# Queries loaded and cast by GpSimd's DMAs, two batches of queries turned by DMAs, and a new order of all events in an attention kernel fused with an ELU network

## The chip, the cores and the metric

The kernel runs on one core of one Trainium2 chip. A core has TensorE (PE in the profile), VectorE (DVE), ScalarE (ACT), GpSimd (POOL) and SyncE (SP), each with its own in-order queue, and 16 DMA engines that all queues share. The metric is the time of one execution on the device, in microseconds; lower is better. It is a median of three runs.

## The reference

Eight batches of eight heads, 576 positions, head size 64. Each batch and head has two attentions that are added, and the sum goes through a two-layer network with ELU.

```
q_d, k_d, v_d = mean over groups of 4 positions of q, k, v      # 144 positions
out_d    = softmax(q_d k_d^T / 8) v_d, each row repeated 4 times
out_local = softmax(q k^T / 8 where |i - j| < 4, else -1e9) v
x = (out_d + out_local) as 4608 tokens x 512
h = x @ w_in                                                    # 512 -> 2048
g = h if h > 0 else exp(h) - 1
y = g @ w_out                                                   # 2048 -> 512
```

## The kernel before

**Tiling.** Heads are taken in pairs, so there are 8 batches b of 4 pairs j. The tokens of the network are cut into 9 blocks t of 512; a batch has 576 tokens, so block t needs batch t and, from block 1 on, the end of batch t - 1.

**Attention of one (b, j).** `lq` loads q and k, `lv` loads v (four DMAs). The data must be 16-bit and have the head size on the partitions. There are three ways for this in the kernel before:

- Batches 0 and 1 (all but the first pair): `load_cast` (line 304). GpSimd issues DMAs that cast on the way, so a 16-bit tile `q16` or `k16` arrives (4 buffers each).
- All others: `load_qk` (line 313). SP issues DMAs of the 32-bit data to `q32` and `k32` (3 buffers each), and `cq` = `cast_qk` (line 335) casts them on GpSimd (line 344), each cast followed by a one-element copy `apart` (line 333).
- From 16 bits on: `tr` = `transposes` (line 399) turns tiles on TensorE into PSUM, and `eq`, `ek` = `evict` (line 422) copy them to `QT`, `KT`. A tile from a casting DMA takes 12 transposes of 64 columns (line 409), a cast tile takes 6 of 128 columns (line 414). From batch `FLIP` = 3 on k is turned by a DMA transpose instead: `fl` = `flip` (line 426), issued by SP. The same for q (`fq`) is written in the code from batch `FLIPQ` on, and `FLIPQ` is 8, so it does not occur.

A load for TensorE's transposes reads runs of 1536 bytes; a load for a DMA transpose reads runs of 256 bytes (`runs_` in `load_qk`).

Then `sq`, `sk` sum groups of four (on DVE, line 443, or in two steps on POOL, lines 447 and 452), `sc` makes the scores, `xl`, `xf` the exponentials (ACT, line 483), `mk` the mask (DVE), `dn` the denominators of a batch (TensorE, line 508), `rc` their reciprocals (DVE, line 518). These are spread over partitions by TensorE in batches 0 to 2 (`sp`, `sx`) and through DRAM in batches 3 to 7 (`so` writes, `si` reads back; both issued by SP). `cv` casts v (POOL), `vs`, `vd` sum it, `out` and `far` multiply with v, `nm` normalises (DVE), and `ad` adds both attentions into the block's input `xt` (line 650, on DVE for the triples in `CFG["adv"]`, else on POOL).

**Network of block t.** `m1.t.i` is one tile of 128 hidden units (4 matmuls of 512 columns, line 663); `ex` and `el` are the ELU, on ACT and DVE: for pairs (t, i) in `CFG["rl"]` two ACT steps and one DVE step (lines 680, 681, 690), else one ACT step and two DVE steps (683, 694, 695). `m2.t.i` is 4 matmuls of the second layer (line 708), `cp` copies and stores. The weights are cast by GpSimd's DMAs as well (`wi`, `wo`, four each of 512 KB).

**What sets the order.** All engines are in order, and the order of their instructions is one written list of events, `ORDER`; each event puts its instructions at the end of its engines' queues. An event written too late in the list comes earlier if something needs it, which is rare here (3 of 1281 events). PSUM tiles of the kind `two` have 3 buffers, and 2 after `cf`. `CFG` says which engine takes which copy, and `fill` how many matmuls on zeros TensorE runs ahead of some events (`keep`, line 394); 13 more stand at the start.

Of the kernel before, what the change touches and what calls it, by code (L numbers as in the profile page):

```python
# [127 lines left out]
lv.1.1 vd.0.0 sp.0.2 sx.0.2 lq.2.0 out.0.0 far.0.0 nm.0.0 ek.1.0 ad.0.0.1 out.0.2 lq.2.3 vs.0.1 vd.0.1
vs.0.3 far.0.2 ad.0.0.0 vd.0.3 sp.0.3 sx.0.3 cf out.0.1 nm.0.2 far.0.1 out.0.3 far.0.3 ad.0.2.0 mp.0.0
mp.1.0 nm.0.1 nm.0.3 ad.0.3.1 ad.0.1.0 mp.0.1 mp.1.1 ad.0.3.0 mp.0.2 mp.0.3 mp.1.2 sk.1.0 m1.0.0 ex.0.0  # L130
mp.1.3 m1.0.1 el.0.0 ex.0.1 el.0.1 tr.1.1 tr.1.3 m1.0.2 eq.1.1 ek.1.3 sq.1.1 ex.0.2 eq.1.3 m1.0.3 ek.1.1
sc.1.0 el.0.2 sq.1.3 m1.0.4 ex.0.3 el.0.3 m1.0.5 cq.2.1 xl.1.0 xf.1.0 cv.1.0 wi.3 ex.0.4 ex.0.5 tr.1.2
# [797 lines left out]
```

## Time and profile before

| what | value |
|---|---|
| median of 3 runs (lowest to highest) | 342.64 us (340.46 to 343.32) |
| the profiled execution's own time | 342.38 us |
| its span, first to last instruction | 340.6 us |
| mean granted TensorE clock | 0.99 |

The page is one profiled execution. Its first part gives each engine's busy time; its second cuts the span in 40 slices of 8.5 us and shows the busy share of each in tenths. Matmuls overlap, so TensorE's busy time is not all work at full rate. The groups by line give the mean duration of one instruction, and the idle time of the engine just before it. The chain of waits follows the work that ended last back from the end.

### The profile page before, as it was taken

Reading aid. Unit: us, or ns where it says so; the run is one execution under the profiler, and the core shown is the slowest. Engines: PE = TensorE matmul, PEld = TensorE weight load, DVE = VectorE, ACT = ScalarE, POOL = GpSimd, SP = SyncE. Lnnn points to the kernel's source line nnn. Section 1 sums busy time; section 2 is a strip of 40 time slices with the busy share of each in tenths; the row PEclk is TensorE's granted clock in tenths of the full one; section 3 lists DMA queues with packets and bytes.
Section 4 is the critical chain, followed back from the end, with each engine's and each line's share of the span. In section 5 each row is a group of like instructions: output and inputs, shape, how many; then the busy total and the mean of one; then the engine's idle time right before and its main releaser. Section 6 shows DMA issues by size and latency. Waiting matters only on the chain.

```text
span 340.6 us, 9762 instructions
## 1 busy us (share of the span) xinstructions
PE 325.0 (95%) x3976; PEld 169.8 (50%) x3976; DVE 230.7 (68%) x429; ACT 209.4 (61%) x365; POOL 156.5 (46%) x299
## 2 busy tenths in 40 slices
PE   6799979999999997999999999999999999999996
PEld 3355445555545553555555555555444444444443
DVE  2668998768778957788997966699775455443400
ACT  3544888888457862555676767765446646657621
POOL 6694765876795674857684347632011000000000
PEclk9879999999999999999999999999999999999999
DMA  8999999989887949999996996331310100000112
GB/s 168 195 180 227 168 248 224 196 196 155 214 149 165 232 114 179 249 199 224 166 251 152 162 239 169 115 88 69 89 64 31 63 34 31 31 33 31 56 70 92
DMA packets 99735, 48.66 MB, mean 143 GB/s; under 512 B 81130, under 2 KB 94698, under 8 KB 99690
## 3 DMA queue, kind: packets, MB, share of 16 engines
q1 hardware_dynamic: 93530, 41.57, 55.1%
q0 software_dynamic: 5600, 6.26, 11.4%
q8 instruction: 31, 0.51, 0.7%
q10 hardware_dynamic: 560, 0.21, 0.3%
q14 instruction: 14, 0.11, 0.1%
HBM read 41.66 MB, written 9.67 MB: 151 GB/s over the span
## 4 chain that ended last, share of the span: by engine, by line
PE 66%; DMA 15%; DVE 8%; ACT 3%; SPq 3%; issue 2%; POOL 1%; ACTq 0%; POOLq 0%; DVEq 0%
PE op L708 28%; PE hp L663 28%; DMA v<-in_v_dram 4%; DMA rcb<-rd 3%; DMA k<-in_k_dram 3%; DMA kt<-k 3%; DVE gt L695 2%; PE lg L592 2%; DVE rc L518 1%; SPq L427 1%; PE sc L463 1%; DVE e L694 1%; DVE ln L643 1%; DMA MASK<-MASKc 1%; PE den L508 1%
## 5 line engine op out<-in xcount | busy, mean ns | idle before, releaser
L663 PE MATMUL hp<-xt,WI 128*128 128x512 f16 x576 | 148.0, 380 | 2.5 <-DVE gt L695 2.2
L708 PE MATMUL op<-WO,gt 128*128 128x512 f16 (+2 forms) x592 | 145.3, 374 | 0.0
L663 PEld LDWEIGHTS <-WI 128*128 128x128 f16 x576 | 62.6, 114 | 57.3 <-issue 3.6
L708 PEld LDWEIGHTS <-gt 128*128 128x128 f16 x592 | 55.1, 98 | 60.2
L690 DVE SCALAR_TENSOR_TENSOR gt<-e,hp 128x512 f16<-128x512 f16 x71 | 48.4, 683 | 43.0 <-ACT e L681 42.6
L683 ACT ACTIVATE e<-hp 128x512 f16<-128x512 f32 x73 | 43.6, 599 | 41.5 <-PE hp L663 40.0
L680 ACT ACTIVATE r<-hp 128x512 f32<-128x512 f32 x71 | 42.6, 600 | 40.9 <-PE hp L663 40.5
L695 DVE SCALAR_TENSOR_TENSOR gt<-hp,e 128x512 f16<-128x512 f32 x73 | 50.5, 692 | 2.8
L650 POOL TENSOR_TENSOR xt<-ln 128x320 f16<-128x320 f16 (+7 forms) x35 | 25.8, 750 | 44.9 <-DVE ln L643 44.8
L681 ACT ACTIVATE e<-r 128x512 f16<-128x512 f32 x71 | 44.7, 630 | 2.2
L483 ACT ACTIVATE pex<-sc 128x580 f16<-128x580 f32 (+1 forms) x64 | 35.2, 591 | 11.3 <-PE sc L473 11.2
L694 DVE TENSOR_SCALAR e<-e 128x512 f16<-128x512 f16 x73 | 27.3, 374 | 20.3 <-ACT e L683 20.2
L386 POOL CAST v<-v 128x640 f16<-128x640 f32 x32 | 23.6, 738 | 13.4 <-DMA v<-in_v_dram 7.2
L716 ACT COPY os<-op 128x512 f32<-128x512 f32 (+2 forms) x37 | 21.1, 573 | 12.6 <-PE op L708 12.3
L643 DVE TENSOR_TENSOR ln<-lg,rcb 128x580 f16<-128x580 f32 x32 | 24.1, 752 | 0.0
L344 POOL CAST k<-k 96x768 f16<-96x768 f32 x24 | 19.6, 818 | 9.1 <-DMA k<-in_k_dram 9.1
L447 POOL TENSOR_TENSOR t<-qt 128x288 f32<-128x288 f16 x19 | 12.8, 672 | 23.6 <-ACT qt L424 13.1
L492 DVE TENSOR_TENSOR pex<-pex,MASK 128x580 f16<-128x580 f16 x32 | 19.6, 626 | 2.4 <-ACT pex L483 2.2
L344 POOL CAST q<-q 96x768 f16<-96x768 f32 x24 | 19.6, 817 | 0.0
L424 ACT COPY qt<-tqk 128x576 f16<-128x576 f16 x18 | 11.5, 637 | 5.9 <-PE tqk L414 5.0
L447 POOL TENSOR_TENSOR t<-kt 128x290 f32<-128x290 f16 x17 | 11.9, 703 | 6.8 <-DMA kt<-k 5.4
L638 DVE TENSOR_TENSOR ln<-lg,rcb 128x144 f16<-128x144 f32 x32 | 9.6, 300 | 7.7 <-PE lg L611 3.7
(71 smaller groups left out, 292.6 us busy)
## 6 DMA issues: line engine op xcount, KB each, us to landing
v<-in_v_dram SPq DMA_DIRECT2D x126, 80.0 KB, 4.2
out_dram<-os SPq DMA_DIRECT2D x35, 256.0 KB, 2.7
q<-in_q_dram SPq DMA_DIRECT2D x25, 288.0 KB, 4.9
k<-in_k_dram SPq DMA_DIRECT2D x25, 288.0 KB, 5.0
rcb<-rd SPq DMA_DIRECT2D x10, 362.0 KB, 5.4
WI<-in_moe_w_in_dram POOLq DMA_DIRECT2D x4, 512.0 KB, 10.7
WO<-in_moe_w_out_dram POOLq DMA_DIRECT2D x4, 512.0 KB, 7.5
q<-in_q_dram POOLq DMA_DIRECT2D x7, 144.0 KB, 6.8
```

The source lines that it names most:

```text
L344: nc.gpsimd.tensor_copy(out=x[:], in_=src)
L483: nc.scalar.activation(out=s["p"][:, :, a : a + n], in_=g2(s["sc"], a, n), func=AF.Exp, scale=SCALE / 16 if far else SCALE,)
L643: nc.vector.tensor_tensor(**near)
L650: eng.tensor_tensor(out=xt(t)[:, j, t0 - TBLK * t : t1 - TBLK * t], in0=ln[:, a:z], in1=_rep4(ln[:, ga : ga + (z - a) // 4]), op=AB.add,)
L663: nc.tensor.matmul(hps[(t, fc)][:], w_in(dc, fc), xts[t][:, dc, :], start=(dc == 0), stop=(dc == DMC - 1),)
L680: nc.scalar.activation(out=r[:], in_=hp[:], func=AF.Relu, scale=-1.0)
L681: nc.scalar.activation(out=e[:], in_=r[:], func=AF.Exp, scale=-1.0)
L683: nc.scalar.activation(out=e[:], in_=hp[:], func=AF.Exp)
L690: nc.vector.scalar_tensor_tensor(out=gts[t][:, fc, :], in0=e[:], scalar=-1.0, op0=AB.add, in1=hp[:], op1=AB.max)
L694: nc.vector.tensor_scalar(out=e[:], in0=e[:], scalar1=1.0, scalar2=-1.0, op0=AB.min, op1=AB.add)
L695: nc.vector.scalar_tensor_tensor(out=gts[t][:, fc, :], in0=hp[:], scalar=0.0, op0=AB.max, in1=e[:], op1=AB.add)
L708: nc.tensor.matmul(op_[:, a:z], gts[t][:, fc, 128 * tt : 128 * tt + 128], WO[fc // 4][:, fc % 4, a:z], start=(fc == 0), stop=(fc == FCN - 1),)
```

## The change

- `is_cast` now holds for batch 2 as well: q and k of batch 2 come by casting DMAs of GpSimd.
- `is_cast_q` holds for batches 3 to 5: q comes by a casting DMA of its own event `lc`, while `lq` loads k alone on SP, and `cq` casts k alone.
- `FLIPQ` is 6: q of batches 6 and 7 is loaded in runs of 256 bytes and turned by DMA transposes (`fq`, SP); it has no `tr` and no `eq`.
- The tables of engines, `adv` (29 entries to 20), `rl` (71 to 55), `fill` (31 matmuls to 30) and the whole list `ORDER` are other ones.

```diff
-FLIPQ = 8
+CASTQ = 6
+FLIPQ = 6
...
- 'eq': {0: 'DDAD', 2: 'DAAD', 4: 'AADD', 5: 'DDDA', 6: 'ADAA', 7: 'AADA', -1: 'DAAA'},
- 'ek': {1: 'ADAA', -1: 'AAAA'},
- 'sq': {1: 'DPDP', 2: 'DPPP', 3: 'PDDD', 4: 'PPPP', 5: 'PPDP', 6: 'DPDP', -1: 'DPPD'},
- 'sk': {0: 'PDDD', 1: 'DDPD', 2: 'PDPP', 4: 'DDDP', 6: 'DPDP', 7: 'DPPP', -1: 'PPDP'},
- 'vd': {0: 'AADA', 3: 'D', 5: 'D', 6: 'D', -1: 'A'},
- 'sx': {2: 'DAAD', -1: 'AAAA'},
+ 'eq': {1: 'AADA', 2: 'AAAD', 3: 'DAAD', 4: 'ADAA', 5: 'DADA', -1: 'AAAA'},
+ 'ek': {1: 'ADAA', -1: 'DAAA'},
+ 'sq': {1: 'DPDP', 2: 'PPPD', 5: 'PPPD', 6: 'DPPP', 7: 'DDPP', -1: 'PPDD'},
+ 'sk': {0: 'DDDD', 3: 'DDPD', 4: 'PPPD', 5: 'PDDP', 6: 'PDPD', -1: 'DPPP'},
+ 'vd': {0: 'AADA', 4: 'D', 5: 'D', -1: 'A'},
+ 'sx': {1: 'DAAA', 2: 'DDAD', -1: 'DADA'},
...
- 'fill': {('sc', 0, 0): 5,
-          ('sc', 0, 1): 3,
-          ('dn', 0, 0): 5,
-          ('sc', 0, 3): 2,
-          ('dn', 0, 1): 4,
-          ('sp', 0, 2): 2,
-          ('out', 0, 0): 3,
+ 'fill': {('sc', 0, 0): 4,
+          ('dn', 0, 0): 7,
+          ('sp', 0, 0): 2,
+          ('out', 0, 0): 5,
+          ('sp', 0, 1): 4,
           ('mp', 0, 0): 3,
-          ('mp', 1, 0): 2,
-          ('sc', 1, 0): 1,
-          ('sp', 1, 2): 1},
+          ('mp', 1, 0): 1,
+          ('dn', 1, 0): 2,
+          ('sp', 1, 2): 2},
...
     def is_cast(b, j):
-        return b < 2 and (b, j) != (0, 0)
+        return b < 3 and (b, j) != (0, 0)
+
+    def is_cast_q(b):
+        return 3 <= b < CASTQ
...
         for src, name in ((q, "q"), (k, "k")):
+            if name == "q" and is_cast_q(b):
+                got.append(None)
+                continue
...
-        got = []
+        got = qk16.setdefault((b, j), [None, None])
         for t, name in list(zip(qk32.pop((b, j)), ("q16", "k16")))[:: 1 if b < FLIP else -1]:
+            if t is None:
+                continue
...
-                if is_cast(b, j):
+                if is_cast(b, j) or (n == 0 and is_cast_q(b)):
...
+            if is_cast_q(b):
+                n32, q16 = n32[1:], n16[:1]
+                n16 = n16[1:]
+                at(("lc", b, j), load_cast, b, j, (0,), alloc=q16)
```

Three places of `ORDER`, where the events that the text names are kept and the others are left out. The start:

```
before: lq.0.1 ... lq.0.3 ... lq.0.2 sel ... sk.0.0 ... lq.1.0 ... cv.0.0 sq.0.1 ... sc.0.1 ... dn.0.0
after:  lq.0.1 ... lq.0.2 ... lq.0.3 ... sq.0.0 ... sq.0.1 sel sc.0.1 ... lq.1.0 ... cv.0.0 ... dn.0.0
```

Batch 2's loads among the weights and the blocks of the network:

```
before: lq.2.1 ... wi.2 ... lq.2.0 ... lq.2.3 ... wi.3 ... wo.0 lq.2.2 ... wo.1 ... wo.2 ... wo.3 ... tr.2.0 ... tr.2.2
after:  wi.2 ... lq.2.1 ... wi.3 ... lq.2.3 wo.0 ... wo.2 ... wo.1 ... lq.2.0 wo.3 ... lq.2.2 ... tr.2.0 ... tr.2.2
```

The denominators of batch 3 and the last q of batch 4:

```
before: cp.1.4 ... lv.5.0 dn.3.0 rc.3.0 ... so.3 ... fl.4.2 ... si.3 ... out.3.2 ... nm.3.2
after:  lv.5.0 ... fl.4.3 ... fl.4.2 tr.4.0 ... cp.1.0 ... dn.3.0 ... cp.1.4 ... rc.3.0 ... so.3 sk.4.0 lc.4.2
        lv.5.3 ... sc.4.3 ... sc.4.0 ... m2.1.10 m1.2.14 ... m2.1.11 ... si.3 lv.5.1 tr.4.2 ... out.3.2 ... nm.3.2
```

More of the change, by code (lines that the diff above doesn't have):

```diff
@@ L128 @@
[L128 to L132, printed above, removed]
@@ new lines @@
+lq.1.0 tr.0.3 eq.0.3 sq.0.3 cv.0.0 lv.1.3 ek.0.3 eq.0.2 xf.0.1 mk.0.0 dn.0.0 sk.0.3 cv.0.2 wi.0 lq.1.3
+lv.1.1 lq.1.2 lq.1.1 sc.0.3 xl.0.3 sq.0.2 rc.0.0 sc.0.2 mk.0.3 sp.0.0 vs.0.2 vs.0.0 xl.0.2 mk.0.2 xf.0.3
+xf.0.2 tr.1.0 vd.0.2 vd.0.0 cv.0.3 lv.1.2 wi.1 wi.2 cv.0.1 sx.0.0 dn.0.1 out.0.0 rc.0.1 lq.2.1 sp.0.2
+far.0.0 eq.1.0 sq.1.0 ek.1.0 sp.0.1 sx.0.1 nm.0.0 out.0.2 vs.0.3 sx.0.2 vs.0.1 ad.0.0.0 far.0.2 nm.0.2
+sp.0.3 vd.0.1 vd.0.3 out.0.1 far.0.1 nm.0.1 out.0.3 sx.0.3 cf ad.0.2.0 ad.0.1.0 far.0.3 ad.0.0.1 nm.0.3
@@ new lines @@
+el.2.13 sk.4.1 sk.4.2 xl.4.0 xf.4.0 xf.4.3 ex.2.14 sq.4.1 si.3 lv.5.1 tr.4.2 sc.4.1 m1.2.15 m2.1.12 xt.5
+eq.4.2 out.3.2 lq.5.2 sq.4.2 xl.4.1 xf.4.1 out.3.3 far.3.2 far.3.3 el.2.14 lq.5.0 m2.1.13 ex.2.15 nm.3.2
+lv.5.2 out.3.1 far.3.1 nm.3.3 m2.1.14 nm.3.1 out.3.0 sc.4.2 ad.3.2.3 cv.5.3 ad.3.2.4 far.3.0 lc.5.1 cv.5.0
+lq.5.1 m2.1.15 cp.1.8 m2.2.0 ad.3.3.3 nm.3.0 ad.3.0.3 ad.3.1.3 xl.4.2 el.2.15 m1.3.0 m2.2.1 cv.5.1 lc.5.2
+cq.5.2 mk.4.2 mk.4.1 ex.3.0 el.3.0 cv.5.2 m1.3.1 m2.2.2 m1.3.2 mk.4.3 vs.5.0 cp.1.12 xf.4.2 ex.3.1 mk.4.0
@@ new lines @@
+cv.7.1 m2.4.10 xl.7.1 xf.7.3 lv.7.2 cv.7.2 out.6.0 lv.7.0 xf.7.1 out.6.2 far.6.0 far.6.2 ex.5.13 cv.7.0
+mk.7.3 m1.5.14 m2.4.11 mk.7.1 cp.4.4 dn.7.0 cp.4.8 nm.6.2 nm.6.0 vs.7.0 m2.4.12 ex.5.14 out.6.3 vd.7.0
+out.6.1 far.6.3 far.6.1 m2.4.13 el.5.13 el.5.14 m1.5.15 xt.8 nm.6.1 ad.6.2.6 ad.6.2.7 ad.6.0.6 ad.6.1.6
+m2.4.14 nm.6.3 ad.6.3.6 m1.6.0 ex.5.15 m2.4.15 ex.6.0 el.5.15 m1.6.1 rc.7.0 out.7.0 out.7.2 ex.6.1 el.6.0
+el.6.1 m1.6.2 m2.5.0 m1.6.3 m2.5.1 cp.4.12 ex.6.2 el.6.2 ex.6.3 el.6.3 m1.6.4 ex.6.4 el.6.4 m2.5.2 m1.6.5
@@ new lines @@
+m2.5.3 m1.6.6 m2.5.4 ex.6.5 el.6.5 ex.6.6 el.6.6 ad.6.0.7 ad.6.1.7 m1.6.7 m2.5.5 m1.6.8 ex.6.7 far.7.2
+far.7.0 m2.5.6 el.6.7 m1.6.9 so.7 si.7 m2.5.7 nm.7.2 ad.7.2.7 ad.7.2.8 nm.7.0 out.7.1 out.7.3 far.7.1
+far.7.3 ex.6.8 ex.6.9 cp.5.0 m2.5.8 ad.6.3.7 el.6.8 m1.6.10 m2.5.9 el.6.9 m1.6.11 m2.5.10 nm.7.1 ex.6.10
+el.6.10 ex.6.11 el.6.11 m1.6.12 ex.6.12 el.6.12 ad.7.0.8 nm.7.3 ad.7.3.7 m2.5.11 m1.6.13 ad.7.0.7 cp.5.4
+m2.5.12 m1.6.14 m2.5.13 ex.6.13 ex.6.14 el.6.13 el.6.14 m1.6.15 cp.5.8 m2.5.14 ad.7.1.7 m1.7.0 ex.6.15
@@ L212 @@
+cp.7.12 m2.8.4 m2.8.5 m2.8.6 m2.8.7 cp.8.0 m2.8.8 m2.8.9 m2.8.10 m2.8.11 cp.8.4 cp.8.8 m2.8.12 cp.8.12
+m2.8.13 cp.8.13
 """
```

163 lines of the change are left out of this document (72 added, 91 removed), and 12 rows, old and new, of the table CFG.

## The prediction

> **What bounds the kernel now.** I read the page's busy times and slices first, then busy time in stretches.
>
> ```profile
> PE 325.0 (95%) x3976; PEld 169.8 (50%) x3976; DVE 230.7 (68%) x429; ACT 209.4 (61%) x365; POOL 156.5 (46%) x299
> DMA  8999999989887949999996996331310100000112
> ```
>
> ```profile
> 0.00:20.00 20.00, 15.00 (x216) 7.55 (x216) 9.38 (x32) 7.82 (x13) 13.56 (x28) 0.86 1.14 184
> 20.00:40.00 20.00, 19.01 (x392) 10.99 (x390) 16.54 (x38) 12.89 (x25) 13.24 (x25) 0.97 1.16 194
> 40.00:60.00 20.00, 17.52 (x355) 10.15 (x349) 18.59 (x36) 16.10 (x28) 13.29 (x26) 1.00 1.09 227
> ...
> 120.00:140.00 20.00, 17.79 (x302) 9.23 (x301) 14.22 (x26) 8.72 (x17) 12.56 (x21) 1.00 0.79 159
> ```
>
> A stretch's columns are PE, PEld, DVE, ACT, POOL busy, then granted clock, DMA share, GB/s. TensorE is the bound: it is busy for 95% of the span. Idle time that a new order could win back stands in two places. The first 60 us hold 5.0 + 1.0 + 2.5 = 8.5 us of idle TensorE, and 120 to 140 another 2.2. The front has more to win than its idle time, because part of its busy time is filler:
>
> ```profile
> L394 PE MATMUL sc<-Z 128*128 128x512 f16 x24 | 8.0, 475 | 1.2 <-DVE v L764 1.2
> ```
>
> That row alone is 8.0 us of matmuls on zeros, all in the front. The DMA engines are 8 or 9 tenths busy in nearly every slice of the first 200 us, so the front is a race of loads, not of TensorE alone. Two views show what the front waits for, the chain of waits and SP's timeline:
>
> ```profile
> 14.19 0.62 POOL t L447
> ...
> 15.36 0.40 PE sc L473 x6
> 15.76 2.25 PE den L394 x5
> ```
>
> ```profile
> 15.00 4.67 SPq L358 DMA_DIRECT2D v<-in_v_dram  x7
> ...
> 23.18 16.77 SPq L358 DMA_DIRECT2D v<-in_v_dram  x12
> 40.05 0.56 SPq L321 DMA_DIRECT2D q<-in_q_dram  x1
> ```
>
> The second scores wait for POOL's sum of q (`sq.0.1`), which stands behind the cast of the first v on POOL, and it is part of the chain. And SP's v loads, 0.67 us each at 15 us (4.67 / 7), take 1.40 us each from 23 us on (16.77 / 12): the issue itself is held up, and batch 2's q waits behind them until 40.05.
>
> **The change, part by part.** The sum is made against the profiled execution, 342.38 us (span 340.6, 1.8 around it), which is 0.26 under the median.
>
> *POOL, DVE, ACT.*
>
> ```profile
> L650 POOL TENSOR_TENSOR xt<-ln 128x320 f16<-128x320 f16 (+7 forms) x35 | 25.8, 750 | 44.9 <-DVE ln L643 44.8
> L344 POOL CAST q<-q 96x768 f16<-96x768 f32 x24 | 19.6, 817 | 0.0
> L333 POOL COPY apart<-q 1x1 f16<-1x1 f16 x24 | 5.2, 215 | 1.5
> L308 POOL DMA_DIRECT2D q<-in_q_dram x7 | 4.7, 668 | 0.9 <-POOLq L914 0.9
> L680 ACT ACTIVATE r<-hp 128x512 f32<-128x512 f32 x71 | 42.6, 600 | 40.9 <-PE hp L663 40.5
> L681 ACT ACTIVATE e<-r 128x512 f16<-128x512 f32 x71 | 44.7, 630 | 2.2
> L683 ACT ACTIVATE e<-hp 128x512 f16<-128x512 f32 x73 | 43.6, 599 | 41.5 <-PE hp L663 40.0 <-DVE gt L695 1.4
> L690 DVE SCALAR_TENSOR_TENSOR gt<-e,hp 128x512 f16<-128x512 f16 x71 | 48.4, 683 | 43.0 <-ACT e L681 42.6
> L694 DVE TENSOR_SCALAR e<-e 128x512 f16<-128x512 f16 x73 | 27.3, 374 | 20.3 <-ACT e L683 20.2
> L695 DVE SCALAR_TENSOR_TENSOR gt<-hp,e 128x512 f16<-128x512 f32 x73 | 50.5, 692 | 2.8
> ```
>
> POOL loses 20 casts with their `apart` (8 tiles of batch 2, 12 q of batches 3 to 5): 20 x (0.817 + 0.215) = 20.6 us. It gets 20 DMA issues, 20 x 0.668 = 13.4, and 9 more `ad`, 9 x 0.750 = 6.8: net -0.4, so POOL's load is moved, not lowered. That costs nothing directly: 44.8 us of its idle time waits for DVE's `ln`. Sixteen ELU tiles leave `rl`: ACT loses 16 x (0.600 + 0.630 - 0.599) = 10.1 us, DVE gains 16 x (0.374 + 0.692 - 0.683) = 6.1, and the nine `ad` (at most POOL's 0.750 each) give back up to 6.8. None is on the path where TensorE is full; they count in the front, where DVE is 18.59 of 20 us busy between 40 and 60. There, between `m1.0.2` and `m1.1.0`, the new list has on DVE three sums, one mask, one `ad` and one ELU step fewer, one eviction and one spread copy more: four instructions fewer, 4 x 0.374 to 4 x 0.692 by the rows above, 1.5 to 2.8 us. DVE is not the path all of that time, so I take 1.0; from a loss of 1 (the sums are POOL's now and may come late) to a gain of 2.
>
> *TensorE's own work.*
>
> ```profile
> 39.13 0.63 PE tqk L409 x24
> ...
> 65.12 0.51 PE tqk L414 x12
> 65.64 0.86 PE hp L663 x4
> ...
> 95.01 0.26 PE tqk L414 x6
> ```
>
> A pair of batch 2 goes from the 0.51 us form to the 0.63 us form: 4 x 0.12 = +0.5. Twelve q of batches 3 to 5 go from 0.26 to half of 0.63: 12 x 0.055 = +0.7. Eight q of batches 6 and 7 leave: -8 x 0.26 = -2.1. One filler less: 8.0 / 24 = -0.3. Sum -1.2 us, where TensorE is full, so on the path. I take all of it (0 to -2: the evictions that go with it free PSUM sooner).
>
> *The front's order.* `sq.0.1` now stands ahead of `lq.1.0` and the cast of v on POOL, and all `sk.0` are on DVE. The piece 14.19 to 15.36 then can't hold the scores, and the next bound is the eviction and the two fillers more ahead of `dn.0.0` (7 instead of 5; 2.25 / 5 = 0.45 each, 0.9 us). Batch 2's q and k leave SP's held-up queue, so its loads no longer wait until 40.05, and SP's v loads have less before them. From 14.19 to 15.36 is 1.2 us, and with what batch 1 wins from a shorter SP queue, less a part of the fillers, I take 1.5; 0 to 3, since the DMA share in the first three stretches is above 1 and the bytes are the same.
>
> *Batch 3's spread.*
>
> ```profile
> 119.85 4.10 SPq L358 DMA_DIRECT2D v<-in_v_dram  x4
> 124.05 0.56 SPq L529 DMA_DIRECT2D rd<-rc  x1
> ```
>
> ```profile
> 126.89 5.70 DMA rcb<-rd
> ```
>
> `lv.5.0` stands right before `so.3` on SP and holds it from 119.85 to 124.05; the landing at 132.6 is what the 2.2 us of idle TensorE in 120 to 140 wait for. In the new list `lv.5.0` stands a block earlier and `lv.5.3` (four issues, 4 x 0.67 = 2.7 us) between `so.3` and `si.3`, where SP waits for the write anyway. I take 1.0 of the 2.2; -1 to +2, for what is late next is `tr.4.2` (first rival).
>
> *SP.* Twenty loads fewer, 20 x 0.56 = 11.2 us; eight transposes more:
>
> ```profile
> L427 SPq DMA_TRANSPOSE kt<-k x20: 1197/1265/2854, 78.6 to 211.1; - x20
> ```
>
> 8 x 1.265 = 10.1 us. The sum is even, but it moves late: seven transposes now stand in the block of `m1.4`, with 25 v issues instead of 12. What hides it is that batches 6 and 7 are loaded early, and that the DMA row of the slices falls to 3 tenths and less from the 26th slice, 213 us, on; with that cover gone it costs what the second rival says.
>
> Sum: 342.4 - 1.0 - 1.2 - 1.5 - 1.0 = 337.7, rounded to 338.
>
> **A rule against it.** GpSimd's casting DMAs issued while DVE is busy are few in this trace, all of weights:
>
> ```profile
> 46.22 0.58 POOL L290 DMA_DIRECT2D WO<-in_moe_w_out_dram  x1
> ```
>
> In the stretch 40 to 60, where DVE is 93% busy, the issue took 0.58 us, no more than the 0.668 of the issues in the first 20 us, where DVE has 9.38 of 20. The Trainium skill's page "SBUF — State Buffer", section "SBUF: two separate sides", says that while VectorE runs an operation in a two-port mode GpSimd can't write descriptors, and gives about 3.1 us for such a DMA that takes 0.62 alone. By that rule, as an estimate from the page, the 20 new DMAs would cost up to 20 x 2.5 = 50 us of waiting; the row speaks against it.
>
> **Rivals.**
>
> *Casts that come too late (slower).* Casting DMAs share GpSimd's software queue with the weights, in order.
>
> ```profile
> DMA to landing us min/median/max: 4.3/6.8/9.9
> ```
>
> ```profile
> WI<-in_moe_w_in_dram POOLq DMA_DIRECT2D x4, 512.0 KB, 10.7
> ```
>
> (The first is for line 308, q and k.) Between `lc.4.2` and `tr.4.2` TensorE has three groups of 4 matmuls, 3 x 0.86, and two scores of less than a group each, 2.6 to 4.3 us; taken as 3.4 against a landing of 6.8, that is 3.4 us of stall. `lq.2.2` stands behind all four `wo` with nine groups, 9 x 0.86 = 7.7 us, ahead of `tr.2.2`; landing like a weight (10.7) it is 3.0 late, and everything of batch 2 with it, which eats the front's 2.5. 342.4 - 1.2 + 3.4 + 3.0 = 347.6. It decides where POOL reaches the issue less than 6.8 us before TensorE wants the tile. For: POOL is in order, and `lc.4.2` stands behind two sums that need `tr.4.0`. Against: POOL has idle time and may run ahead.
>
> *SP late in batches 6 and 7 (slower).* 13 more v issues and three more transposes in that block, 13 x 0.67 + 3 x 1.265 = 12.5 us; if half of it isn't hidden, with the front's gain, 342.4 - 2.5 - 1.2 + 6.2 = 345, and 349 without that gain.
>
> *Nothing but TensorE's work (same).* The new order wins as much as it loses: 342.4 - 1.2 = 341.
>
> *Issues that VectorE holds up (slower).* If a busy DVE blocked GpSimd's issue, each of the 20 could be late by up to the weights' landing over the casts', 10.7 - 6.8 = 3.9 us, and with half of them in TensorE's way it is 342.4 + 39 = 381. It is the rule above as a mechanism here; the 0.58 us row leaves it little.
>
> **How the numbers follow.** Forecast 0.43, casts late 0.25, SP late 0.11, only TensorE's work 0.18, issues held up 0.03. I call 1% (339.2 to 346.1 around the median) what a measurement of this kernel can tell from no change. The forecast's terms at their bad ends give 342.4 + 1 + 1 = 344.4, at their good ends 342.4 - 2 - 2 - 3 - 2 = 333.4; of its 0.43, 0.37 lies under 339.2 and 0.06 within. TensorE's work alone gives 0.03 faster, 0.14 within, 0.01 slower; SP late 0.03 within and 0.08 slower; late casts 0.02 within and 0.23 slower. So faster 0.40, same 0.25, slower 0.35. The range 332 to 350 holds the forecast's good end and both likelier slower rivals. It leaves out 0.03 for held-up issues, 0.08 for slower rivals that add up, and 0.08 for a front that wins more than I see. The forecast alone: 333 to 344.
>
> **What would show it.** Front: `m1.1` starts on TensorE some 2 us sooner, and the chain no longer has POOL's `qd` ahead of the second scores. Casts: no wait of `tqk` for a DMA of q in batches 2 to 5; a TensorE gap ahead of `tr.4.2` or `tr.2.2` shows the first rival. Spread: `rd` issued within 2 us of `rc`. SP: line 427 with 28 transposes whose end doesn't hold up `si` of batches 5 to 7. The prediction is wrong if TensorE's idle time in the first 60 us stays at 8.5 us or grows, or if new idle time of over 3 us appears between 60 and 240.

## The result and the profile after

The changed kernel takes 353.1 us (median of 5 runs, 350.68 to 355.28) against 341.73 of the kernel before (5 runs, 340.46 to 343.32): a ratio of 1.033, interval 1.027 to 1.040. The forecast was 338 and the range ended at 350. The profiled execution took 353.1 us, with a span of 351.3, which is 10.7 more than the 340.6 of before. Medians are of all runs of a kernel; ratios and their intervals leave out single runs over 1.5% above its fastest.

The page of the changed kernel, then its busy time in stretches (columns as before):

```profile
PE 323.3 (92%) x4047; PEld 166.7 (47%) x4047; DVE 237.4 (68%) x426; ACT 196.3 (56%) x343; POOL 155.2 (44%) x288
DMA  8999599949686899896986897896130100100112
```

```profile
0.00:20.00 20.00, 14.86 (x307) 8.71 (x308) 10.93 (x35) 11.22 (x20) 14.76 (x31) 1.00 1.00 175
20.00:40.00 20.00, 13.21 (x231) 6.92 (x228) 13.75 (x22) 6.76 (x14) 9.60 (x16) 0.83 1.15 180
40.00:60.00 20.00, 17.50 (x340) 9.62 (x337) 16.94 (x31) 14.90 (x26) 16.89 (x33) 1.00 0.86 155
...
120.00:140.00 20.00, 16.86 (x349) 9.16 (x347) 13.50 (x22) 13.07 (x24) 9.13 (x18) 1.00 1.12 197
```

TensorE has less to do (323.3 against 325.0 us) and waits longer. In the first 60 us it is idle for 5.1 + 6.8 + 2.5 = 14.4 us, where it was 8.5. Nearly all of the increase lies between 20 and 40, where the granted clock is 0.83 too: it was half from 28.2 to 35.0 us, and the network's first matmuls fell into that stretch. Before, the half-clock stretch lay from 14.5 to 21.3, ahead of them.

To place the loss, the times at which `m1.0.2` and then the first tile of each later block start on TensorE cut every execution into a front, stages 0 to 5 (from one block's first tile to the next) and the rest. In the expectations "first m1 matmul" is the first of these marks.

| us | front | 0 | 1 | 2 | 3 | 4 | 5 | rest |
|---|---|---|---|---|---|---|---|---|
| before | 34.2 | 26.4 | 35.4 | 41.4 | 35.8 | 30.5 | 34.2 | 102.7 |
| after | 37.8 | 27.6 | 37.3 | 42.5 | 35.6 | 30.1 | 37.1 | 103.3 |

The loss is 3.6 + 1.2 in front and stage 0, 1.9 and 1.1 in stages 1 and 2, 2.9 in stage 5 and 0.6 in the rest; stages 3 and 4 give back 0.6. TensorE's idle time grew by 6.0 in the front (part of the front's work moved out of it), 1.1 and 1.2 in stages 1 and 2 and 3.1 in stage 5. In stage 0 it did not grow (2.8 before, 2.7 after): that stage is longer because TensorE has more of its own work there, 96 transposes of four head pairs in place of 36 of two.

What TensorE waited for, from the table of waits (total, number, longest) of the changed kernel, and the row of the kernel before that answers to the first:

```profile
PE vs L569 <- POOL v L389: 5.7, 3, 2.0
PE hp L397 <- DVE ln L646: 4.1, 1, 4.1
```

```profile
PE vs L566 <- POOL v L386: 0.6, 2, 0.4
```

Two new waits, then: for casts of v (in the front, stage 2 and stage 5), and once, in the front, 4.1 us for VectorE. The front of the changed kernel on GpSimd (start, duration, instruction, and the idle time before it):

```profile
15.44 0.77 POOL L282 DMA_DIRECT2D WI<-in_moe_w_in_dram  x1
16.21 0.64 POOL L307 DMA_DIRECT2D q<-in_q_dram  x1
...
22.84 0.75 POOL L282 DMA_DIRECT2D WI<-in_moe_w_in_dram  x1 [1.05 <-DMA WI<-in_moe_w_in_dram]
25.34 0.72 POOL L389 CAST v<-v 128x640 f16<-128x640 f32 x1 [1.75 <-DMA v<-in_v_dram]
...
27.93 3.36 POOL L653 TENSOR_TENSOR xt<-ln 128x512 f16<-128x512 f16 x4
```

GpSimd reaches its loads early and then stands before the last v tile of batch 0, which has not landed. VectorE, in the changed kernel and in the kernel before:

```profile
28.51 2.63 DVE L653 TENSOR_TENSOR xt<-ln 128x64 f16<-128x64 f16 x1
31.27 0.31 DVE L641 TENSOR_TENSOR ln<-lg,rcb 128x144 f16<-128x144 f32 x1
```

```profile
28.02 0.23 DVE L650 TENSOR_TENSOR xt<-ln 128x64 f16<-128x64 f16 x1
```

The same small add, `ad.0.0.1`, takes 2.63 us in place of 0.23. It ends at 28.51 + 2.63 = 31.14, just behind the third of GpSimd's four adds (31.05; three of 128x512 at 1.06 to 1.08 us each and one of 128x64), the first of which began 0.6 us ahead of it; before, it began 0.06 us ahead of GpSimd's first. The next normalisation, `nm.0.3`, stands behind it.

### The profile page after: what moved, and what is told of

It is laid out like the page before. It is cut to its first block, busy times and chain, and to the rows that moved or that the text cites. A ratio compares the mean times of both kernels' runs of the same rounds, so it can differ in the third digit from the quotient of the medians.

```text
span 351.3 us, 9853 instructions
## 1 busy us (share of the span) xinstructions
PE 323.3 (92%) x4047; PEld 166.7 (47%) x4047; DVE 237.4 (68%) x426; ACT 196.3 (56%) x343; POOL 155.2 (44%) x288
## 4 chain that ended last, share of the span: by engine, by line
PE 61%; DMA 13%; DVE 13%; SPq 4%; POOL 3%; ACT 2%; issue 2%; DVEq 0%; POOLq 0%; ACTq 0%
PE op L711 27%; PE hp L666 26%; DMA v<-in_v_dram 6%; DMA rcb<-rd 3%; DVE gt L698 3%; DVE e L697 3%; SPq L361 2%; DVE ln L646 2%; DVE xt L653 2%; DVE pex L495 2%; PE lg L595 2%; DMA k<-in_k_dram 1%; SPq L430 1%; DMA q<-in_q_dram 1%; DMA rd<-rc 1%
## 5 line engine op out<-in xcount | busy, mean ns | idle before, releaser
L686 ACT ACTIVATE e<-hp 128x512 f16<-128x512 f32 x89 | 53.2, 598 | 63.9 <-PE hp L666 61.7
L698 DVE SCALAR_TENSOR_TENSOR gt<-hp,e 128x512 f16<-128x512 f32 x89 | 61.6, 692 | 3.3
L693 DVE SCALAR_TENSOR_TENSOR gt<-e,hp 128x512 f16<-128x512 f16 x55 | 37.5, 682 | 33.9 <-ACT e L684 33.8
L697 DVE TENSOR_SCALAR e<-e 128x512 f16<-128x512 f16 x89 | 35.0, 394 | 30.2 <-ACT e L686 30.0
L653 POOL TENSOR_TENSOR xt<-ln 128x512 f16<-128x512 f16 (+7 forms) x44 | 31.0, 719 | 51.4 <-DVE ln L646 43.8
L683 ACT ACTIVATE r<-hp 128x512 f32<-128x512 f32 x55 | 33.0, 600 | 36.9 <-PE hp L666 36.9
L486 ACT ACTIVATE pex<-sc 128x580 f16<-128x580 f32 (+1 forms) x64 | 35.4, 596 | 10.6 <-PE sc L476 10.6
L684 ACT ACTIVATE e<-r 128x512 f16<-128x512 f32 x55 | 34.7, 632 | 1.8
L719 ACT COPY os<-op 128x512 f32<-128x512 f32 (+2 forms) x37 | 20.9, 570 | 14.1 <-PE op L711 14.1
L348 POOL CAST k<-k 96x768 f16<-96x768 f32 x20 | 16.5, 826 | 10.2 <-DMA k<-in_k_dram 10.2
L307 POOL DMA_DIRECT2D q<-in_q_dram x23 | 15.1, 655 | 2.2 <-POOLq L921 0.9
L653 DVE TENSOR_TENSOR xt<-ln 128x256 f16<-128x256 f16 (+7 forms) x20 | 14.0, 714 | 0.2
```

The lines of the kernel that those rows point to most:

```text
L486: nc.scalar.activation(out=s["p"][:, :, a : a + n], in_=g2(s["sc"], a, n), func=AF.Exp, scale=SCALE / 16 if far else SCALE,)
L653: eng.tensor_tensor(out=xt(t)[:, j, t0 - TBLK * t : t1 - TBLK * t], in0=ln[:, a:z], in1=_rep4(ln[:, ga : ga + (z - a) // 4]), op=AB.add,)
L683: nc.scalar.activation(out=r[:], in_=hp[:], func=AF.Relu, scale=-1.0)
L684: nc.scalar.activation(out=e[:], in_=r[:], func=AF.Exp, scale=-1.0)
L686: nc.scalar.activation(out=e[:], in_=hp[:], func=AF.Exp)
L693: nc.vector.scalar_tensor_tensor(out=gts[t][:, fc, :], in0=e[:], scalar=-1.0, op0=AB.add, in1=hp[:], op1=AB.max)
```

## The experiments

All ratios are to the kernel before, run on the same chip between the others (medians of 341.1 to 342.4 us there). A single profile places a wait well but a mark badly: four kernels with the changed kernel's front untouched (the changed one, d3, c1, c2) have their first mark at 36.2 to 40.2 us, and stage 5 took 34.2 to 39.5 where nothing in it was edited. So the readings go by waits.

**First question: the loads or the order?** Four kernels put parts of the change into the old order and the old tables. a1 takes batch 2 by casting DMAs (`is_cast` for b < 3, its four `lq.2` at new places), a2 q of batches 3 to 5, a3 turns q of batches 6 and 7 by DMAs, a4 does all three.

```diff
a1
-        return b < 2 and (b, j) != (0, 0)
+        return b < 3 and (b, j) != (0, 0)
-lq.2.1 ... sq.1.0 ... lq.2.0 ... lq.2.3 ... sq.1.3 ... eq.1.2 ... cv.1.2 ... lq.2.2
+sq.1.0 lq.2.1 ... sq.1.3 lq.2.0 ... eq.1.2 lq.2.3 ... cv.1.2 lq.2.2
a2
+CASTQ = 6
-cq.3.2 ...
+lc.3.2 cq.3.2 ...
a3
-FLIPQ = 8
+FLIPQ = 6
-fl.6.1 ... fl.7.0 ... fl.6.3 ... si.5
+fl.6.1 fq.6.1 ... fl.7.0 fq.7.0 ... fl.6.3 fq.6.3 ... si.5
```

> The kernel before with one part alone: q and k of batch 2 by casting DMAs of GpSimd, the old order and tables, with the four loads of batch 2 put where their tiles come free. Theory 'order' (the new order and tables cost the 11 us, the three loading changes nothing): within 1% of 342, likely 341 to 342, since POOL loses 3 us of work and TensorE gains 0.5. Theory 'loads' (the casting DMAs collide with v and weights): slower by 2 to 4 us, with the loss in the first 70 us.

> The kernel before with q of batches 3 to 5 by casting DMAs alone, each issued where its cast stood. Theory 'order': 341 to 343 (TensorE +0.7 to +1.2, POOL 4 us less). Theory 'loads': 345 or more, with TensorE waiting for q's landing ahead of its transposes between 80 and 170 us.

> The kernel before with q of batches 6 and 7 turned by DMA transposes alone, each right behind k's. Theory 'order': 340 to 341 (TensorE loses 2.1 us of transposes on its full path). Theory 'loads' (SP and the DMA engines late for batches 6 and 7): 343 to 346, with the loss after 150 us.

> All three loading changes in the old order and tables. Theory 'order': the sum of the three, 340 to 342. Theory 'loads': near the changed kernel, 349 to 353.

| kernel | us | ratio (interval) | front | 0 | 1 | 2 | 3 | 4 | 5 |
|---|---|---|---|---|---|---|---|---|---|
| a1 | 341.64 | 1.003 (0.999 to 1.007) | 34.1 | 25.7 | 35.7 | 40.1 | 35.9 | 30.9 | 34.2 |
| a2 | 341.73 | 1.003 (0.999 to 1.007) | 33.0 | 26.3 | 35.9 | 39.8 | 36.7 | 30.3 | 34.2 |
| a3 | 352.44 | 1.030 (1.021 to 1.038) | 33.5 | 26.1 | 35.4 | 42.1 | 36.4 | 38.6 | 36.0 |
| a4 | 353.22 | 1.034 (1.028 to 1.040) | 34.5 | 25.6 | 36.1 | 40.4 | 39.0 | 37.2 | 35.7 |

In the old order the casting DMAs cost nothing that can be told (0.7% at most). The eight DMA transposes alone cost as much as the whole change, but in other places: stages 4 and 5 lose 8.1 and 1.8 in a3, and -0.4 and 2.9 in the changed kernel. So it is chance that a4 and the changed kernel take the same time: the old order loses some 10 us to the transposes and next to nothing in the first blocks, the new order loses 2.5 in these two stages and 3.6 + 1.2 + 1.9 + 1.1 = 7.8 ahead of them, which the loads alone, in the old order, do not cost. SP's timeline of a3 shows where its 8 us come from, with VectorE's longest wait:

```profile
182.75 1.25 SPq L434 DMA_TRANSPOSE kt<-k  x1
184.09 1.22 SPq L434 DMA_TRANSPOSE qt<-q  x1
...
189.36 1.22 SPq L434 DMA_TRANSPOSE qt<-q  x1
190.67 1.88 SPq L542 DMA_DIRECT2D rcb<-rd  x2
192.61 7.81 SPq L365 DMA_DIRECT2D v<-in_v_dram  x11
```

```profile
DVE ln L645 <- DMA rcb<-rd: 6.5, 1, 6.5
```

Six transposes of 1.2 us each, three before, go ahead of `si.5`, the load of batch 5's spread (190.67; before 184.70). VectorE waits 6.5 us for it, and TensorE's gap of 6.5 us ahead of `sc.6.1` ends as this normalisation, `nm.5.2`, ends and frees its PSUM (198.9); the table of waits names a load of v there, which scores don't read. The granted clock is then half from 196.5 to 203.3, and four first-layer matmuls take 1.90 us in it, in place of 1.03, so the gap costs more than its own length.

**The transposes in the old order.** f1 puts `si.5` and, on VectorE, `nm.5.1` ahead. f2 is f1 with the v loads of batches 6 and 7 issued by GpSimd. f3 puts the four transposes behind `lv.6.0` as well.

```diff
a3: fl.7.0 fq.7.0 ... fl.6.3 fq.6.3 ... si.5 ... lv.6.1 ... sk.7.0 ... lv.6.0 ... sq.7.0 ... nm.5.1
f1: si.5 fl.7.0 fq.7.0 fl.6.3 fq.6.3 ... lv.6.1 ... lv.6.0 ... nm.5.1 sk.7.0 sq.7.0
f3: si.5 ... lv.6.1 ... lv.6.0 fl.7.0 fq.7.0 fl.6.3 fq.6.3 ... nm.5.1 sk.7.0 sq.7.0
f2, besides f1:
-            nc.sync.dma_start(
+            (nc.gpsimd if b >= 6 else nc.sync).dma_start(
```

> The kernel of a3_flip_q (the old kernel with q of batches 6 and 7 turned by DMAs) with si.5, the load of batch 5's spread, ahead of four of the six transposes that held it, and sk.7.0 and sq.7.0 behind nm.5.1 on VectorE. Theory spread: the 6.6 us gap at 192 is nm.5.2 waiting for si.5, issued at 190.7 in place of 184.7; with the load issued at about 186 stage 4 falls from 38.6 to 31 to 33, time 345 to 347. Theory whole queue: the v loads behind the transposes are as late, the gap moves to vs.6 or to the scores and the time stays above 350.

> The kernel of f1_spread_ahead with all v loads of batches 6 and 7 issued by GpSimd (32 issues of about 0.65 us, 21 us of an engine that is busy 6.5 of 20 us at 180 to 200). Theory whole queue: with SP free of them stages 4 and 5 return to the old 30.5 and 34.2 less TensorE's 8 x 0.26 us: 339 to 342, level with or ahead of the old kernel. Theory spread alone: like f1, within 1 us. If GpSimd's issues hold its casts and sums: above f1.

> The kernel of a3_flip_q with the four transposes of batch 7's first and batch 6's last head pair behind si.5, lv.6.1 and lv.6.0 in SP's queue, and sk.7.0 and sq.7.0 behind nm.5.1. Theory order: SP has the time and only its order was wrong; neither nm.5.2 nor vs.6.0 waits, stage 4 is back at 30 to 31.5 us, time 343 to 345. Theory total: the seven us of issues that q's transposes add before 201 us make whatever is last late; sc.7.0 (200.5 us in the old kernel) or vs.6.0 waits 3 to 5 us instead, stage 4 stays above 34 and the time above 347.

The longest wait behind each edit, f1 and f2 around 200 us, f3 around 235:

```profile
PE vs L573 <- POOL v L393: 4.1, 1, 4.1
```

```profile
PE vs L573 <- POOL v L393: 7.6, 1, 7.6
```

```profile
DVE ln L645 <- DMA rcb<-rd: 4.7, 1, 4.7
...
PE lg L599 <- DVE ln L650: 4.1, 1, 4.1
```

f1: 351.15 us (1.030, 1.026 to 1.034). The wait for the spread is nearly gone (the gap ahead of `sc.6.1` falls from 6.5 to 1.4), and 4.1 us for v stand in its place. f2: 356.84 (1.044, 1.040 to 1.049): on GpSimd's queue v is later still. f3: 353.6 (1.032, 1.022 to 1.041): `vs.6.0` waits 0.3, but a sum of batch 7 on VectorE waits 1.7 for its transpose, TensorE 2.1 for the ELU step behind that sum, stage 4 still takes 36.3, and the next batch's spread is 4.7 late. In the old order each place tried for the eight issues makes something else late; an order that has room was not found.

**The front.** b1 moves the small add on VectorE away from GpSimd's; b2 moves three casting loads behind GpSimd's add `ad.0.1.0`; b12 does both. d1 is b1 with the weights `wi` later. e12 is b1 with all six of GpSimd's loads behind the last v cast (and the v loads of stage 5 below). g1 puts the weights between the casts of v and the casting loads behind the adds; g2 is g1 with the load that g1 waits for put forward.

```diff
after: cv.0.2 wi.0 lq.1.3 ... lq.1.2 lq.1.1 ... cv.0.3 ... wi.1 wi.2 cv.0.1 ... lq.2.1 ... nm.0.0 ... ad.0.1.0 far.0.3 ad.0.0.1 nm.0.3
b1:    nm.0.0 ad.0.0.1 ... ad.0.1.0 far.0.3 nm.0.3
b2:    cv.0.2 wi.0 lq.1.3 ... cv.0.3 ... wi.1 wi.2 cv.0.1 ... ad.0.1.0 lq.1.2 lq.1.1 lq.2.1 far.0.3 ad.0.0.1 nm.0.3
d1:    cv.0.2 lq.1.3 ... lq.1.2 lq.1.1 wi.0 ... cv.0.3 ... cv.0.1 wi.1 wi.2 ... lq.2.1 ... ad.0.1.0
e12:   cv.0.2 ... cv.0.3 ... cv.0.1 wi.0 wi.1 wi.2 lq.1.3 lq.1.2 lq.1.1 ... lq.2.1 ... ad.0.1.0
g1:    cv.0.2 ... cv.0.3 wi.0 ... cv.0.1 wi.1 wi.2 ... ad.0.1.0 lq.1.3 lq.1.2 lq.1.1 lq.2.1
g2:    cv.0.2 ... cv.0.3 wi.0 ... cv.0.1 lq.1.3 wi.1 wi.2 ... ad.0.1.0 lq.1.1 lq.1.2 lq.2.1
```

> The changed kernel with one event moved: the add ad.0.0.1 (VectorE) right behind nm.0.0, ahead of GpSimd's four adds instead of beside them. Theory lock: that add took 2.63 us in place of 0.23 because GpSimd's adds ran at the same time; first m1 matmul from 37.8 to about 35.4 us, the gap of 4.24 us at 28.0 to about 2, time 2.4 us less than the changed kernel's (about 350.7). Theory chain: the gap is set by GpSimd's adds themselves (they begin late, behind the v cast), so the mark moves by less than 0.7 us and the time stays at 353.

> The changed kernel with three casting DMAs (lq.1.1, lq.1.2, lq.2.1) moved behind the add ad.0.1.0. Theory collision: the last v part of batch 0 landed 8.45 us after its issue because these transfers and the first WI lay on the same DMA engines, and the issues kept GpSimd from its adds; the v cast then ends about 2 us sooner, the gap of 2.19 us at 23.9 goes, first m1 matmul at 35.3 to 35.8, time about 351. Theory queue: the last v part is late because SP issues it late; it lands at 25 as before, the mark moves by less than 0.7 us, and batch 1's scores become later (stage 0 some 1 us longer).

> Both moves together. If lock and collision are two losses one after the other, the sum: first m1 matmul at about 33.5 to 34 us, at the old kernel's 34.2 or ahead of it, time about 349. If they cover the same wait, no better than the better of the two (about 351). If neither holds: 353.

> The kernel of b1_add_early with the three loads of the WI moved behind: wi.0 behind lq.1.1, wi.1 and wi.2 behind the v cast cv.0.1. Theory weights: the last v part of batch 0 lands 6.5 to 8 us after its issue, where the old kernel's took 5, because wi.0 (512 KB) is issued 3.5 us sooner and lies with it on the DMA engines; with it behind, cv.0.1 begins at 22.5 to 23 in place of 24.0, the gap of 1.5 us at 23.2 goes and the first m1 matmul comes at 34 to 34.3, time about 349.3. Theory rows: v lands late whatever lies beside it, because its own packets are slow (SP's issue ends at 17.4); cv.0.1 stays at 24, and the m1 stage may wait for a WI that lands later: 350 to 352.

> The kernel of b1_add_early with two edits in different stages. Front: the three WI loads and the casting DMAs lq.1.1, lq.1.2, lq.1.3 all behind the v cast cv.0.1. Stage 5: the v loads lv.7.2 and lv.7.0 issued by GpSimd instead of SP, behind lv.7.1 in the order. Theory collision: with v alone on the DMA engines its last part lands within 5 us of its issue's end (6.6 to 8.6 in six kernels of this order), cv.0.1 begins at 21.5 to 23, and the first m1 matmul comes at 33 to 34.5; theory own packets: 6.5 us or more again, mark at 35 or later. Theory SP: with eight issues off SP, neither the gap ahead of vs.7 nor one ahead of sc.7 is left, stage 5 takes 34 to 35 us in place of 36 to 39; theory order: 36 or more. Both yes: about 347; batch 1's later loads may give back up to 2 us in stage 0.

> The kernel of b1_add_early with wi.0 behind cv.0.3, wi.1 and wi.2 behind cv.0.1, and the casting DMAs lq.1.1, lq.1.2, lq.1.3, lq.2.1 behind the add ad.0.1.0. Theory collision and issue limit: cv.0.1 begins at 21 to 22.5 as in e12_front_and_v7 (20.9), GpSimd's adds follow without a wait, mp.0.0 at 27 to 28.5 and the first m1 matmul at 32 to 34; stage 0 may take 1 us more, time 347 to 349. Rival: WI lands 11 us after its issue, so that m1 waits for it until 33 to 36 whatever v does: first m1 matmul at 36, time 350 to 351.

> The kernel of g1_front_loads with lq.1.3 put forward, right behind cv.0.1, and lq.1.1 ahead of lq.1.2. Theory places of loads: the wait of 4.95 us ahead of tr.1.3 goes, mp.0.0 stays at 27.4 to 28.5 and the first m1 matmul comes at 31.5 to 33, ahead of the old kernel's 34.2; time 347 to 348.5, that is 5 us less than the changed kernel's, with the rest of the loss in the stages behind. Rival: another load of the front is then the late one (lq.1.1 ahead of tr.1.1, or a WI), the first m1 matmul or stage 0 gives back more than 3 us, and the time is 350 or more.

| kernel | us | ratio (interval) | `cv.0.1` starts | `mp.0.0` starts | front | end of stage 0 |
|---|---|---|---|---|---|---|
| before | 341.73 | | 24.8 | 30.4 | 34.2 | 60.6 |
| after | 353.1 | 1.033 (1.027 to 1.040) | 25.3 | 33.6 | 37.8 | 65.4 |
| b1 | 350.31 | 1.022 (1.016 to 1.029) | 24.0 | 30.1 | 35.3 | 64.2 |
| b2 | 351.54 | 1.025 (1.018 to 1.032) | 26.1 | 32.5 | 36.7 | 63.9 |
| b12 | 349.95 | 1.023 (1.017 to 1.028) | 27.2 | 33.4 | 38.3 | 65.8 |
| d1 | 352.74 | no interval | 25.7 | 32.8 | 37.9 | 66.6 |
| e12 | 363.41 | 1.066 (1.058 to 1.074) | 20.9 | 39.6 | 44.1 | 71.2 |
| g1 | 352.48 | 1.032 (1.024 to 1.039) | 20.5 | 27.4 | 36.3 | 65.8 |
| g2 | 352.71 | 1.031 (1.022 to 1.039) | 20.6 | 27.8 | 31.2 | 64.8 |

The add, in b1:

```profile
22.58 0.23 DVE L651 TENSOR_TENSOR xt<-ln 128x64 f16<-128x64 f16 x1
```

From `cv.0.1` to `mp.0.0` it is 8.2 us in all five profiles with the add beside a run of GpSimd's (after, c1, c2, d2, d3) and 6.2 in b1 and b12: there it costs 2.0. b2 agrees: the add is in its old place, but falls into a pause between GpSimd's adds, takes 0.21 us, and from the cast to `mp.0.0` it is 6.4. The gain does not last to the end of stage 0, which is 40.1 us behind the start of `cv.0.1` in the changed kernel and 40.2 in b1. In b1 the granted clock was half from 24.3 to 34.5, and seven first-layer matmuls took 3.19 us there, 1.87 in the kernel before; and VectorE's next add, of 128x512, now met GpSimd's (1.38 us in place of 0.69). The Trainium skill's page "SBUF — State Buffer", section "SBUF: two separate sides", says that VectorE and GpSimd share a port pair as an exclusive lock for a whole instruction, which a VectorE operation with two SBUF inputs needs against a GpSimd operation that reads SBUF. The trace agrees (2.63 us against 0.23), and goes further, since the add did not get in behind the first of GpSimd's adds either, nor behind the second.

The second loss is the v tile. Its cast starts only 0.5 us later than before (25.3 against 24.8), so what it takes is the lead that GpSimd had by then. With half of the other transfers moved (b2, d1) it is as late as ever, and both expectations missed; with all of them behind it (e12), or all but one weight load that was issued 0.8 us ahead of the cast (g1, g2), the cast starts at 20.5 to 20.9 us in place of 23.3 to 27.3. So they collide, and either half seems to be enough. In e12 a new wait showed, on GpSimd:

```profile
20.87 0.72 POOL L387 CAST v<-v 128x640 f16<-128x640 f32 x1 [1.00 <-DMA v<-in_v_dram]
...
28.81 0.63 POOL L305 DMA_DIRECT2D k<-in_k_dram  x1 [1.53 <-DMA WI<-in_moe_w_in_dram]
32.15 0.63 POOL L305 DMA_DIRECT2D q<-in_q_dram  x1 [2.70 <-DMA WI<-in_moe_w_in_dram]
35.54 0.63 POOL L305 DMA_DIRECT2D k<-in_k_dram  x1 [2.76 <-DMA WI<-in_moe_w_in_dram]
36.19 3.82 POOL L651 TENSOR_TENSOR xt<-ln 128x512 f16<-128x512 f16 x4
```

After eight issues in a row each further one waits for a transfer to land, and the adds wait behind the issues. In g1 the adds go first and `mp.0.0` starts at 27.4, ahead of both kernels. Then TensorE waits for batch 1's q, `lq.1.3` in g1 and `lq.1.1` in g2:

```profile
PE tqk L410 <- DMA q<-in_q_dram: 4.8, 1, 4.8
```

```profile
PE tqk L410 <- DMA q<-in_q_dram: 4.5, 1, 4.5
```

g2 has the first mark 3 us ahead of the kernel before and has lost it all by the end of stage 0: behind this wait its granted clock is half from 36.1 to 42.9. That mark lies at 63.3 to 71.2 in the twelve profiles of the new order and at 59.2 to 60.6 in the eight of the old one. The placement of the loads is thus a cause, but no placement tried here won the front back. The ratios of b1, b2 and b12 (1.022 to 1.025) lie some 1% under the changed kernel's 1.033, with intervals that overlap, and b12 has its gain in stage 5 (34.2), where nothing was edited.

**Stages 1, 2 and 5.** d2 gives the changed kernel the old table `rl`. d3 puts `lv.7.2` and `lv.7.0` right behind `lv.7.1`; e12 has them there too, issued by GpSimd. c1 and c2 turn q of batches 6 and 7 on TensorE again (`FLIPQ` = 8), c1 with `tr` and `eq` right ahead of `sq`, c2 with them in the place of `fq`.

```diff
after: lv.7.1 lq.7.3 ... fl.7.2 ... fq.7.2 fl.7.1 ... fq.7.1 ... fq.7.3 ... fl.7.3 ... si.6 ... lv.7.2 ... lv.7.0
d3:    lv.7.1 lv.7.2 lv.7.0 lq.7.3 ... fl.7.2 ... fq.7.2 fl.7.1 ... fq.7.1 ... fq.7.3 ... fl.7.3 ... si.6
c1:    ... tr.6.0 eq.6.0 sq.6.0 ...
c2:    ... tr.6.0 eq.6.0 fl.6.0 ... sq.6.0 ...
```

> The changed kernel with the old table of which blocks take the two-step way of the activation (71 entries in place of 55; 9 in place of 6 in the second m1 stage), nothing else. Theory table: the new table leaves VectorE more of the work where it already limits, so the second m1 stage (65.4 to 102.7, 37.3 us) falls back to 35.4 to 36 and the time to about 351.5. Theory order: the stage's length comes from where the order puts the attention of batches 2 and 3; it stays within 0.5 us of 37.3 and the time at 353, or rises, since the order was made for the new table.

> The changed kernel with the last two v loads of batch 7 (lv.7.2 and lv.7.0) moved ahead in SP's queue, right behind lv.7.1, ahead of seven DMA transposes. Theory SP: the wait of 1.9 us ahead of vs.7 at 241 comes from loads issued behind those transposes; it goes, and stage 5 falls from 37.1 to 34.2 to 35.2, time about 351. If the transposes so put back make the scores of batch 7 late, a new gap ahead of sc.7 of the same size appears and the time stays at 353. Theory order alone: stage 5 stays at 36 to 37 and no scores are later.

> The changed kernel with q of batches 6 and 7 turned by TensorE again (eight transposes and copies placed ahead of sq), the rest of its order kept. Theory SP: the eight DMA transposes of q keep SP's queue full in stages 4 and 5, so v of batch 7 is issued late; the gaps of stage 5 (0.7, 1.0, 1.9 us) go and stage 5 is 2 to 3 us shorter, against 8 x 0.26 us more of TensorE and some 2 us of copies: about 351 to 352. Theory order alone: stage 5 stays at 37 us, and the time rises by TensorE's 2 us to about 355.

> The changed kernel with q of batches 6 and 7 turned by TensorE, each transpose and its copy at the place in the order where the changed kernel has the DMA transpose, so that they aren't just ahead of their use as in c1_flip_k_only. Theory SP: SP's queue is eight issues shorter between 173 and 229; the gaps of stage 5 (0.7, 1.0, 1.9 us) go, stages 4 and 5 together fall from 67.2 to about 65, against 8 x 0.26 us more of TensorE: 351 to 352.5. Theory order: the copies are added to VectorE and ScalarE in two stages whose order left no room for them, each waits in turn as in c1_flip_k_only, and the time is 356 or more.

d2: 357.61 us (1.042, 1.033 to 1.051), stage 1 at 38.5, so in this order the old table does not win stage 1 back. What the profile shows of stage 1, where TensorE's idle time grew from 0.4 to 1.5 us, is VectorE's short ELU step, by form between 60 and 100 us, before and after:

```profile
L694 DVE TENSOR_SCALAR e<-e 128x512 f16<-128x512 f16 x9 | 3.9, 438 | 3.0 <-ACT e L683 3.0
```

```profile
L697 DVE TENSOR_SCALAR e<-e 128x512 f16<-128x512 f16 x11 | 6.5, 595 | 2.0 <-ACT e L686 2.0
```

It takes longer where GpSimd's casts run back to back (up to 1.35 us at 84.7), which looks like the lock of the front; but the kernel before has casts back to back in this stage too. No run took them away, so for stage 1 this stays an argument. In stage 2 TensorE waits 1.9 us, at 124.8, for a cast of v that stands on GpSimd behind a cast of k, and that one waited 1.7 us for its load. No run tested this either.

d3: 355.31 us (1.035, 1.025 to 1.045). The longest waits at 226 to 240 us, where the changed kernel waited 1.8 for a cast of v at 241:

```profile
DVE qd L444 <- DMA qt<-q: 4.1, 1, 4.1
PE sc L474 <- POOL qd L453: 3.6, 1, 3.6
```

The v loads put forward make the transposes late, as the expectation's second case has it: SP is full here. In the changed kernel it issues without a pause from 219 us to the last v load:

```profile
228.93 2.54 SPq L430 DMA_TRANSPOSE kt<-k  x1
231.57 1.26 SPq L538 DMA_DIRECT2D rcb<-rd  x2
232.88 5.53 SPq L361 DMA_DIRECT2D v<-in_v_dram  x8
```

e12 has those eight issues off SP, and in its stage 5 TensorE no longer waits for v or for batch 7's sums (1.8 and 1.4 us in the changed kernel). But the issues took GpSimd 5.4 us from 212.4, its adds stood behind them, a normalisation on VectorE waited 3.8 us for these, and `vs` for the normalisation:

```profile
PE vs L567 <- DVE ln L644: 3.5, 1, 3.5
```

Behind that gap the granted clock was half from 219.2 to 226.0, and stages 4 and 5 took 34.2 and 37.7, so moving the issues to GpSimd is no cure.

c1 (371.12, 1.085, 1.078 to 1.091) and c2 (376.09, 1.100, 1.090 to 1.110) say nothing of SP: in stage 4 TensorE waits for PSUM, for example, in c1, for a normalisation that has to free it,

```profile
PE sc L465 <- DVE ln L645: 4.8, 1, 4.8
```

because the order leaves no room for eight transposes there. What the change would do with them on TensorE in an order made for it stays open.

## Why the prediction was wrong

**The front's order (-1.5), the step that failed.** Its first half came as forecast: `sq.0.1` no longer holds the scores, and the fillers of `dn.0.0` start at 12.9 in place of 15.7. The step then took this lead through to the end ("with what batch 1 wins from a shorter SP queue"). In fact GpSimd, freed sooner, started loads sooner (the first WI at 15.44 in place of 18.97), and these collided with the last v tile, whose cast then came 0.5 us later than before, with the lead gone; and the adds met VectorE's (2.0 us). In place of -1.5 came +3.6 at the first mark: 0.5 up to that cast, 2.7 on to `mp.0.0` and 0.4 on to the mark. The sign of being wrong that the prediction named came with it: TensorE's idle time in the first 60 us grew from 8.5 to 14.4. The prediction saw a DMA share above 1 in these stretches and used it as a bound of the gain, not as a sign of a loss.

**DVE in the block of m1.0 (-1.0).** What the term counted came: VectorE's busy time in stage 0 fell from 24.7 to 22.6 us, and TensorE waited less for its ELU step (first 66 us, before and after):

```profile
PE hp L663 <- DVE gt L695: 2.2, 6, 0.6
```

```profile
PE hp L666 <- DVE gt L698: 1.3, 4, 0.6
```

Stage 0 grew by 1.2 all the same, by TensorE's own work: transposes of a pair of batch 1 and a pair of batch 2 more stand in it. The sum counted what the transposes cost in all, not in which stage they come.

**The rule of the shared ports.** It was weighed, but only against GpSimd's issues, where it did not bite; between the adds it did. The issues of the changed kernel:

```profile
L307 POOL DMA_DIRECT2D q<-in_q_dram x23 | 15.1, 655 | 2.2 <-POOLq L921 0.9
```

An issue takes 0.655 us as before (0.668), so "issues that VectorE holds up" fell.

**Batch 3's spread (-1.0).** From the end of `rc.3.0` to `nm.3.2` it is 14.7 us, before 14.9. `so.3` came 3.5 us behind `rc.3.0` (before 6.3), not within 2, held by two transposes and two stores; and `si.3` then came 4.0 us behind `so.3`, before 2.2, with four v issues between them.

**TensorE's own work (-1.2).** Right in sign and size: busy time fell by 1.7. Two q-only transposes in a row show the price, 0.35 each where 0.315 was taken:

```profile
93.78 0.70 PE L412 MATMUL tqk<-ID,q 96*64 96x96 f16 x24
```

**POOL's net of -0.4, "costs nothing directly".** The sum was right (155.2 against 156.5 us busy), the conclusion not: where GpSimd's work stands against VectorE's decides, and 2.0 us ahead of `mp.0.0` are that.

**The rivals.** "Casts that come too late" did not happen: a1 and a2 are level, and TensorE waits for no q of batches 2 to 5. "SP late in batches 6 and 7" did, at 2.9 us in stage 5 with the new order (0 to 5.3 in the profiles that share this stage) and some 10 in the old one, against 6.2 forecast; it had 0.11. Its 349 "without that gain" is 347.4 by its own terms, 342.4 - 1.2 + 6.2. The cover named for it (the early loads and the empty DMA slices from 213 us on) was cover for transfers, while what was full was SP's time to issue: 1.2 us for a transpose that before was TensorE's 0.26.

Of the 10.7 us, 3.6 lie in the front. There the 2.0 of the add are shown up to `mp.0.0`, and the v tile's collision is shown, with its repair given back by the next load. Stage 0 (1.2) is read from the counts of TensorE's work, and stages 1 and 2 (3.0) from the waits alone. That SP's issues are what is late is shown for the old order by a3 and f1 to f3, and for stage 5 of the new one by the waits of d3 and e12. TensorE's granted clock was not tested by itself. No version here beats the kernel before; the lowest of the new order is b12 with 349.95.

## What to carry to other kernels

Freeing an engine that also issues loads moves those loads forward: before counting the gain, look up which transfer is due next on the same DMA engines and what stands behind the issues on that engine. Moving work from TensorE to a DMA that one queue issues is paid in that queue's time, and the bill comes at whatever is written last in it. Where each repair moves a wait instead of removing it (spread, then v, then the next spread), the resource is probably full, and another place in the same order is not the cure. And a gap ahead of dense matmuls can cost more than its length: look up the granted clock behind it.

## What the runs showed of the hardware

- A VectorE add of 128x64 took 2.63 us beside GpSimd adds in a row (three of 128x512, one of 128x64), and 0.21 to 0.23 in a pause or started ahead of them; it got in behind the third, not behind the first or second.
- GpSimd's DMA issues of q and k cost 0.63 to 0.67 us each, but in e12, after eight in a row, each waited 1.5 to 2.8 us for a landing and held the arithmetic behind it.
- A DMA transpose held SP's queue for 1.2 us, about as long as two v loads.
- TensorE's granted clock was half for 6.8 us around long gaps: from 28.2 to 35.0 in the changed kernel (gap of 4.1 us up to 32.3), from 196.5 to 203.3 in a3 (6.5 up to 199.0), from 219.2 to 226.0 in e12 (3.5 up to 220.3). In a3 four matmuls of 512 columns took 1.90 us there in place of 1.03.
